# Attention products of a pair of heads in three runs on the matrix engine instead of four

## The chip, the cores and the metric

The kernel runs on one core of one Trainium2 chip. The metric is the device time of one execution in microseconds. Three executions of the kernel before took 984.92, 981.54 and 982.50 us; the median is 982.5 us.

## What is computed

The output is two results side by side. Result A is an attention with a compressive memory: 2048 positions of 576 features, 32 heads of 18 features, in four segments of 512 positions. Result B is the real part of a two-dimensional Fourier transform, written as products with cosine and sine matrices. Cut to what matters:

```python
for s in range(N):                      # N = 4 segments of L = 512 positions
    logits = qs @ ks.T * scale + mask   # per head, causal
    a_dot = softmax(logits) @ vs
    o = g * (pq @ M) / (pq @ z + 1e-6) + (1 - g) * a_dot
    M, z = M + pk.T @ vs, z + pk.sum()  # pq = phi(qs), pk = phi(ks)
A = concat(o) @ wo
a, b = x @ dft_hid_re.T, x @ dft_hid_im.T
B = dft_seq_re @ a - dft_seq_im @ b     # 2048 x 2048 times 2048 x 576, twice
```

## The kernel before, in words

The program has three stages. The first projects queries, keys and values and keeps the memory sums; the last is the output projection `output_stage`. The stage between them, from about 218 us to 918 us of the trace, holds the change. There the program writes two streams of work into one another by hand.

The **dense stream** is result B, in the generator `dense`. Its matmuls are `d<-wide,chi`, `d<-wide,clo` and the like (L584, and L629 to L634 in `hidden`): stationary blocks of 128x128 and 288 moving columns, both of 4-byte numbers. A high part `chi` is cut by ScalarE and a low part `clo` by GpSimd, and the output tiles `d` have three banks of PSUM.

The **attention stream** is the generator `attention`, one turn for each of the 64 pairs of heads and four more turns to empty the pipeline. Its matmuls have 2-byte operands. Of pair p it handles several ages at once: the even head's score products for the row maxima are made at age 0, the odd head's scores at age 2 (`F_LAG`), the even head's transposed scores at age 3 (`T_LAG`) and the value sums `pv` of both heads at age 4 (`V_LAG`).

- `s_fill(n, kind)`: the even head's score products of one `kind` by `scores` (L969), and the row minima on VectorE by `smallest` (L975), into `negm`. There are three kinds, which together cover the causal triangle: kind 0 is one product of 512 columns, kind 1 is two products of 128 and 384 columns, kind 2 is one product of 256 columns.
- `f_fill(n, kind)`: the same for the odd head, into `nb`; its scores stay in PSUM until `f_exp` reads them on ScalarE. Kind 0 goes to a bank of the tag `t`, the others to a bank of `s`.
- `t_fill(n, kind)`: the even head's transposed scores in a bank of `t` (L1046, L1051, L1055, L1056), and their exponentials on ScalarE. `t_lo` makes the low halves `plo`; of kind 1 it reads the bank itself (L1078, VectorE).
- `pv(n)`: 20 products of 55 and 37 columns for one head (L1095, L1096). The weights are `phi` and `plo` for the even head and the transposed `ptt` for the odd one.

The tags `s` and `t` have two banks each, taken in turn by `bank`. Each new tile must wait until the readers of the bank's last tile are done.

A turn has eight slots. Each slot emits its attention work and then yields a weight from `SLOTS`; the loop that calls it then emits dense matmuls until the dense share of the work has caught up. So the attention products come in **runs**, with dense matmuls between them. In the kernel before a turn has four: slot 2 (`s_fill` 0 and 1, `t_fill` 0 and 1), slot 4 (value sums of the even head, then `s_fill` 2), slot 5 (`f_fill` 1, `t_fill` 2, `f_fill` 0) and slot 7 (value sums of the odd head, then `f_fill` 2). Where the dense stream is ahead, nothing is emitted after slot 4, and the runs of slots 4 and 5 stand together.

Of the kernel before, what the change touches and what calls it, by code (L numbers as in the profile page):

```python
# [12 lines left out]
F32 = mybir.dt.float32  # L13
# [9 lines left out]
S, D, H, DH, NSEG, L = 2048, 576, 32, 18, 4, 512  # L23
P = 128
# [16 lines left out]
def infini_attention_and_fnet(ctx: ExitStack, tc: tile.TileContext, xT, wqk, w8, wv, wo, beta, xtT, cT, hT, out):  # L41
# [46 lines left out]
    def later(n, fn, *a):  # L88
        due.setdefault(clock[0] + n, []).append((fn, a))
# [113 lines left out]
    for i in range(2):  # L203
        kn.append(tuple(sk.tile([P, D], F32R, name=f"kn{n}{i}") for n in "hl"))
        t = sk.tile([P, 2, H, 19], F32R, name=f"vn{i}")
# [3 lines left out]
    for i in range(3):  # L209
        t = sb.tile([P, H, 55], BF16, name=f"vs{i}")  # L210
# [253 lines left out]
    def stacks(p_, i):  # L464
        qs_bufs.append(p_.tile([P, 4, L], BF16, name=f"qs{i}"))
        ks_bufs.append(p_.tile([P, 4, L], BF16, name=f"ks{i}"))
        pool.memset(ks_bufs[i].bitcast(F32)[96:], BF16_ONES)

    CAUSAL, NEGM, MB, OG = [], [], [], []
# [18 lines left out]
    def stack_load(G):  # L488
        if G < NG:
            s, g8 = divmod(G, 8)  # L490
            rows = slice(g8 * 72, g8 * 72 + 72)
            for n, (buf, src) in enumerate(((ks_bufs, kd), (qs_bufs, qd))):
                later(1 + n, dma, buf[G % 4][:NPAIR], src[s][rows].rearrange("(h d) c t -> (d c) h t", d=DH))
# [71 lines left out]
    def bank(name, shape, dtype, tag):  # L565
        turns[tag] ^= 1
        return ps.tile(shape, dtype, name=name, tag=f"{tag}{turns[tag]}", bufs=1)
# [392 lines left out]
    ROWS = (((3, 0),), ((0, 384), (2, 0)), ((1, 0),))  # L960
    FIRST_COL = {3: 0, 2: 512, 0: 896, 1: 1024}

    def scores(n, kind, tag="s"):
        G, h = divmod(n, 4)
        q, k = qs_bufs[G % 4][:NPAIR, h], ks_bufs[G % 4][:NPAIR, h]
        o = bank("s", [P, L], F32, tag)
        for i, c in ROWS[kind]:
            w = (i + 1) * P
            pe.matmul(o[:, c:c + w], q[:, i * P:w], k[:, :w], start=True, stop=True)  # L969
        return o  # L970

    def smallest(o, kind, scale, into):
        for i, c in ROWS[kind]:
            w = (i + 1) * P
            dve.tensor_tensor_reduce(o[:, c:c + w], o[:, c:c + w], CAUSAL[0][:, L - w:], scale=scale, scalar=-LOWEST,  # L975
                                     op0=OP.add, op1=OP.min, accum_out=into[:, i:i + 1])

    def s_fill(n, kind):
        G, h = divmod(n, 4)
        smallest(scores(n, kind), kind, -1.0, NEGM[G % 2][:, 2 * h:2 * h + 4])  # L980

    F_ = {}

    def f_fill(n, kind):
        o = scores(n, kind, "s" if kind else "t")
        if kind == 1:
            F_[n] = [sa.tile([P, 4], F32, name="nb", bufs=2), sa.tile([P, 1280], F32, name="pf", bufs=3), {}]
        smallest(o, kind, -SCALE, F_[n][0])
        F_[n][2][kind] = o
# [28 lines left out]
    def maxima(G):  # L1018
        m, b = NEGM[G % 2].rearrange("p (h n) -> p h n", h=2), MB[G % 2][:, :24].rearrange("p (h c n) -> p c h n", h=2, c=3)
        r = sa.tile([P, 2, 4], F32, name="negx", bufs=2)  # L1020
        pool.tensor_copy(b[:, 0], m)
        pool.tensor_tensor(r, m, b[:, 0], OP.subtract)
        pool.tensor_copy(b[:, 1], r)
        pool.tensor_tensor(b[:, 2], r, b[:, 1], OP.subtract)

    def maxima_transpose(G, o):
        t = o[:, 384:512]
        pe.matmul(t, MB[G % 2], ident16, start=True, stop=True)
        yield
        w = sa.tile([24, P], BF16, name="mt", bufs=2)  # L1030
        act.activation(w, t[:24], AF.Copy)
        for h in range(2):
            later(1, dma, qs_bufs[G % 4][NPAIR:NPAIR + 3, 2 * h].rearrange("c (n t) -> c n t", n=4), w[12 * h:12 * h + 12])
# [64 lines left out]
    def pv_out(n2):  # L1098
        G, hh = divmod(n2, 2)
        s, g8 = divmod(G, 8)  # L1100
        o = PV.pop(n2)
        og = OG[G % 2]
        h0 = 4 * g8 + 2 * hh
        w = o[:, 440:].rearrange("p (h i c) -> p h i c", h=2, c=1)
        b = o[:, :144].rearrange("p (h i d) -> p h i d", h=2, i=4)
        o = o[:, :440].rearrange("p (h i c) -> p h i c", h=2, i=4)
        a = sa.tile([P, 8, DH], F32, name="pa", bufs=2)
        dve.reciprocal(w, o[:, :, :, 54:])
        dve.tensor_tensor(w, w, g1[:, h0:h0 + 2, None, None].to_broadcast([P, 2, 4, 1]), OP.mult)
        dve.tensor_reduce(a, o[:, :, :, :54].rearrange("p h i (c d) -> p (h i) d c", c=3), axis=AX, op=OP.add)  # L1110
        to = og[:, :, 36 * hh:36 * hh + 36].rearrange("p i (h d) -> p h i d", d=DH)
        a = a.rearrange("p (h i) d -> p h i d", h=2)
        if s == 0:
            dve.tensor_tensor(to, a, w.to_broadcast([P, 2, 4, DH]), OP.mult)
        else:
            dve.tensor_tensor(b, a, w.to_broadcast([P, 2, 4, DH]), OP.mult)
            dve.tensor_tensor(to, to, b, OP.add)
        if hh == 1:
            later(6, turn_out, G)
# [33 lines left out]
    F_LAG, T_LAG, V_LAG = 2, 3, 4  # L1153
    NP = 2 * NG
    SLOTS = (1060.0, 890.0, 1060.0, 660.0, 890.0, 1060.0, 650.0, 1210.0)

    def attention():
        for p in range(NP + V_LAG):
            def even(lag, fn, *a):
                if 0 <= p - lag < NP:  # L1160
                    fn(2 * (p - lag), *a)

            def odd(lag, fn, *a):
                if 0 <= p - lag < NP:
                    fn(2 * (p - lag) + 1, *a)

            if p < 2:
                OG.append(sa.tile([P, 4, 72], F32, name=f"og{p}"))
            if p == 0:
                stack_load(1)  # L1170
                later(20, value_load, 0)
            if p % 2 == 0:
                later(39, value_load, p // 2 + 1)
                later(30, memory_load, p // 2)
            even(T_LAG + 1, t_lo, 0)
            odd(F_LAG + 1, f_split_hi)
            yield SLOTS[0]
            G = p // 2 - 1 if p % 2 == 0 and 0 < p <= NP else None
            even(0, s_fill, 0)
            even(T_LAG, t_fill, 0)  # L1180
            even(T_LAG, t_fill, 1, G)
            even(0, s_fill, 1)
            if G is not None and p < T_LAG:
                list(maxima_transpose(G, bank("trm", [P, L], F32, "t")))
            odd(F_LAG + 1, f_split_lo, pool, 512, 1280)
            yield SLOTS[1]
            even(T_LAG, t_lo, 1)
            odd(F_LAG + 1, f_split_lo, dve, 0, 512)
            yield SLOTS[2]
            even(V_LAG, pv)  # L1190
            if p < 2:
                stacks(sq, p + 2)
            even(0, s_fill, 2)
            even(T_LAG, t_mask)
            yield SLOTS[3]
            odd(F_LAG, f_fill, 1)
            even(T_LAG, t_fill, 2)
            odd(F_LAG, f_fill, 0)
            if p % 2 and p < NP:
                maxima(p // 2)  # L1200
            yield SLOTS[4]
            odd(F_LAG + 1, f_turn)
            if p % 2:
                if p == 1:
                    later(6, stack_load, 2)
                else:
                    stack_load((p + 3) // 2)
                if 2 < p < 18:
                    later(2, copy_parts, 2, 7 + p // 2)
            elif 4 <= p < 36:  # L1210
                later(2, copy_parts, 3, (p - 4) // 2)
            even(T_LAG, t_hi)
            yield SLOTS[5]
            odd(V_LAG, pv)
            odd(F_LAG, f_fill, 2)
            odd(F_LAG, f_exp, 1)
            even(T_LAG, t_lo, 2)
            yield SLOTS[6]
            odd(F_LAG, f_exp, 0, 2)
            if V_LAG <= p < NP + V_LAG - 1:  # L1220
                pv_out(p - V_LAG)
            yield SLOTS[7]
# [8 lines left out]
    for n, w in enumerate(attention()):  # L1231
        tick()
        ta += w
        for fn, a in PLAN.pop(n, ()):
            fn(*a)
        while td / total_d < ta / total_a:
            t = next(d, BREAK)
            if t is BREAK:
                break
            td += t  # L1240
# [56 lines left out]
```

## Time and profile before

| | |
|---|---|
| median of three executions | 982.5 us |
| the profiled execution | 981.44 us |
| its span in the trace | 979.7 us |
| busy: TensorE matmuls, weight loads | 974.2 us, 916.4 us |
| busy: VectorE, ScalarE, GpSimd | 742.1 us, 702.2 us, 661.4 us |
| granted TensorE clock | 0.999 of full |

The span is what the trace covers, 1.7 us less than the execution's own time. TensorE's matmuls are listed with a start and a duration; they are pipelined and their ends are modelled, so neighbours overlap in the list and the busy time says little. What counts is the time from one start to another with a known number of matmuls between them.

### The profile page before, as it was taken

To read this page: it belongs to the slowest core of one execution; us is meant where nothing else is said; L and a number is where in the kernel's file an instruction comes from. 1 tells how busy PE (TensorE), PEld (TensorE's weight loads), DVE (VectorE), ACT (ScalarE), POOL (GpSimd) and SP (SyncE) were. 2 spreads that over 40 slices of the span, in tenths; PEclk is the share of its full clock that TensorE was granted. 3 is DMA by queue.
4 is the path that set the end of the run, shared out by engine and by line. 5 is a ranking of instruction groups with operands and counts; after the bars stand their busy time and mean duration, and the time that the engine had idled before them with its cause. 6 is when DMAs were issued, how large, how long until landed. Compare 5 with 4: busy or idle time off the path is not lost.

```text
span 979.7 us, 25347 instructions
## 1 busy us (share of the span) xinstructions
PE 974.2 (99%) x9246; PEld 916.4 (94%) x9246; DVE 742.1 (76%) x2113; ACT 702.2 (72%) x1623; POOL 661.4 (68%) x746
## 2 busy tenths in 40 slices
PE   9999999999999999999999999999999999999998
PEld 8989989899999999999999999999999999999998
DVE  6657668585677767777888777787888798887884
ACT  6757576564877777878878787877777777778442
POOL 2658577686766766677676776667667986677561
PEclk9999999999999999999999999999999999999999
DMA  7537556775777999889999999889999999988662
GB/s 243 197 117 244 200 169 247 236 249 175 203 185 204 217 240 239 220 213 244 222 251 244 236 207 203 184 197 226 233 240 257 249 243 233 226 206 186 174 206 107
DMA packets 304349, 209.95 MB, mean 214 GB/s; under 512 B 204992, under 2 KB 259136, under 8 KB 304192
## 3 DMA queue, kind: packets, MB, share of 16 engines
q1 hardware_dynamic: 304000, 208.20, 82.6%
q8 instruction: 72, 1.18, 0.5%
q14 instruction: 53, 0.43, 0.1%
q10 hardware_dynamic: 224, 0.14, 0.0%
HBM read 122.37 MB, written 58.98 MB: 185 GB/s over the span
## 4 chain that ended last, share of the span: by engine, by line
PE 99%; ACT 0%; DVE 0%; issue 0%
PE d L584 42%; PE s L969 7%; PE v L84 6%; PE qk L84 6%; PE qk L251 6%; PE pv L1095 4%; PE d L629 4%; PE d L630 3%; PE d L631 3%; PE pv L1096 2%; PE t L869 2%; PE d L869 2%; PE s L869 2%; PE t L1046 1%; PE m L364 1%; PE look L397 1%
## 5 line engine op out<-in xcount | busy, mean ns | idle before, releaser
L975 DVE CUSTOM_DVE_ANT_0 s<-s,causal 128x128 f32<-128x128 f32 (+3 forms) x512 | 249.8, 504 | 103.6 <-PE s L969 97.0
L457 POOL TENSOR_TENSOR clo<-craw,chi 128x512 fp32r<-128x512 f32 x159 | 217.0, 1365 | 107.3 <-ACT chi L452 91.9
L584 PE MATMUL d<-wide,chi 128*128 128x288 f32 x1408 | 260.1, 302 | 0.0
L584 PEld LDWEIGHTS d<-wide,chi 128*128 128x128 f32 x1408 | 210.5, 188 | 0.7
L584 PE MATMUL d<-wide,clo 128*128 128x288 f32 x704 | 171.2, 310 | 0.0
L1011 POOL TENSOR_TENSOR hl<-pf,hl 128x768 f16<-128x768 f32 x64 | 107.7, 1683 | 66.7 <-ACT hl L1007 54.2
L969 PE MATMUL s<-ks,qs 108*128 108x128 bf16 (+3 forms) x512 | 131.6, 301 | 0.0
L1059 ACT ACTIVATE phi<-t 128x384 f16<-128x384 f32 x128 | 61.9, 483 | 90.9 <-PE t L1056 90.7
L998 ACT ACTIVATE pf<-s,nb 128x128 f32<-128x128 f32 (+3 forms) x256 | 121.0, 524 | 4.2
L584 PE MATMUL d<-ab,chi 128*128 128x288 f32 x640 | 122.3, 300 | 0.0
L584 PEld LDWEIGHTS d<-wide,clo 128*128 128x128 f32 x704 | 117.7, 188 | 0.9
L452 ACT ACTIVATE chi<-craw 128x512 fp32r<-128x512 f32 x160 | 100.0, 625 | 2.8 <-DMA craw<-cT 1.2
L584 PEld LDWEIGHTS d<-ab,chi 128*128 128x128 f32 x640 | 97.6, 188 | 0.3
L1007 ACT ACTIVATE hl<-pf 128x768 f16<-128x768 f32 (+1 forms) x128 | 87.3, 732 | 1.0
L584 PE MATMUL d<-ab,clo 128*128 128x288 f32 x320 | 82.4, 306 | 0.0
L629 PE MATMUL d<-wide,chi 128*128 128x288 f32 x256 | 79.7, 311 | 0.0
L630 PE MATMUL d<-wide,chi 128*128 128x288 f32 x256 | 75.6, 295 | 0.0
L631 PE MATMUL d<-wide,clo 128*128 128x288 f32 x256 | 75.5, 295 | 0.0
L1063 ACT ACTIVATE pf<-t 128x512 f32<-128x512 f32 (+1 forms) x128 | 68.9, 538 | 1.6 <-PE t L1046 1.4
L1078 POOL TENSOR_TENSOR plo<-pf,phi 128x384 f16<-128x384 f32 x64 | 60.9, 952 | 11.2 <-ACT pf L1063 9.0
L289 POOL TENSOR_TENSOR p<-r,p 128x512 bf16<-128x512 f32 x36 | 43.4, 1209 | 22.2 <-ACT p L288 20.9
L969 PEld LDWEIGHTS <-qs 108*128 108x128 bf16 x512 | 44.3, 97 | 13.8 <-issue 0.2
(286 smaller groups left out, 2584.9 us busy)
## 6 DMA issues: line engine op xcount, KB each, us to landing
craw<-cT SPq DMA_DIRECT2D x128, 256.0 KB
ks<-kd SPq DMA_DIRECT2D x32, 432.0 KB
qs<-qd SPq DMA_DIRECT2D x32, 432.0 KB
craw<-xtT SPq DMA_DIRECT2D x32, 320.0 KB
vd<-vs SPq DMA_DIRECT2D x16, 440.0 KB
vst<-vd SPq DMA_DIRECT2D x32, 220.0 KB
qd<-p SPq DMA_DIRECT2D x16, 384.0 KB
kd<-p SPq DMA_DIRECT2D x16, 384.0 KB
```

The source lines that it names most:

```text
L84: pe.matmul(o, a, b, start=n == 0, stop=n == len(terms) - 1)
L452: act.activation(hi, raw[:, :4], AF.Copy)
L457: engine.tensor_tensor(lo, raw[:, :4], hi.bitcast(F32), OP.subtract)
L584: pe.matmul(o[h], a, b[:, h * 288:h * 288 + 288], start=start, stop=stop)
L629: pe.matmul(o, xh[:, k], wl[k][:, cs], start=k == 0, stop=False)
L630: pe.matmul(o, xh[:, k], wh[k][:, cs], start=False, stop=False)
L631: pe.matmul(o, xl[:, k], wh[k][:, cs], start=False, stop=False)
L969: pe.matmul(o[:, c:c + w], q[:, i * P:w], k[:, :w], start=True, stop=True)
L975: dve.tensor_tensor_reduce(o[:, c:c + w], o[:, c:c + w], CAUSAL[0][:, L - w:], scale=scale, scalar=-LOWEST, op0=OP.add, op1=OP.min, accum_ ...
L998: act.activation(f[:, FIRST_COL[i]:FIRST_COL[i] + w], o[kind][:, c:c + w], AF.Exp, bias=nb[:, i:i + 1], scale=-1.0)
L1007: act.activation(hl[:, 0, a:b], f[:, a:b], AF.Copy)
L1011: engine.tensor_tensor(hl[:, 1, a:b], f[:, a:b], hl[:, 0, a:b], OP.subtract)
```

## The change

Three moves within a turn. The value sums of the even head go from slot 4 to the end of slot 5. The even head's 256 columns (`s_fill` 2) and the odd head's (`f_fill` 2, before in slot 7) go into slot 5 as well, directly after `f_fill` 1, and share one `s` bank: the even head's in its first half, the odd head's in its second. VectorE's minima of the two follow in slot 5. `maxima` goes from slot 5 to slot 6. `SLOTS` is not changed.

```diff
+    SHARED = []
+
     def scores(n, kind, tag="s"):
         G, h = divmod(n, 4)
         q, k = qs_bufs[G % 4][:NPAIR, h], ks_bufs[G % 4][:NPAIR, h]
-        o = bank("s", [P, L], F32, tag)
+        if kind == 2 and SHARED:
+            o = SHARED.pop()
+        else:
+            o = bank("s", [P, L], F32, tag)
+            if kind == 2:
+                SHARED.append(o[:, 256:])
...
             even(T_LAG, t_lo, 1)
             odd(F_LAG + 1, f_split_lo, dve, 0, 512)
             yield SLOTS[2]
-            even(V_LAG, pv)
             if p < 2:
                 stacks(sq, p + 2)
-            even(0, s_fill, 2)
             even(T_LAG, t_mask)
             yield SLOTS[3]
+            SHARED.clear()
+            both = {}
             odd(F_LAG, f_fill, 1)
+            even(0, lambda n: both.update(s=scores(n, 2)))
+            odd(F_LAG, lambda n: both.update(f=scores(n, 2)))
+            even(0, lambda n: s_fill(n, 2, both["s"]))
             even(T_LAG, t_fill, 2)
             odd(F_LAG, f_fill, 0)
+            odd(F_LAG, lambda n: f_fill(n, 2, both["f"]))
+            even(V_LAG, pv)
+            yield SLOTS[4]
             if p % 2 and p < NP:
                 maxima(p // 2)
-            yield SLOTS[4]
             odd(F_LAG + 1, f_turn)
...
             yield SLOTS[5]
             odd(V_LAG, pv)
-            odd(F_LAG, f_fill, 2)
             odd(F_LAG, f_exp, 1)
```

`s_fill` and `f_fill` take the filled bank as an argument where it is given.

**TensorE, end of the run of slot 4, before** (turn 18; `s_6280` is the even head's 256 columns, `d_5996` the dense stream):

```order
L1095 LDWEIGHTS phi_6025
L1095 MATMUL pv_6259<-vst_5982,phi_6025 128x55
L1096 LDWEIGHTS plo_6026
L1096 MATMUL pv_6259<-vst_5982,plo_6026 128x37
L969 LDWEIGHTS qs1_2774
L969 MATMUL s_6280<-ks1_2775,qs1_2774 128x256
L584 MATMUL d_5996<-ab_3830,chi_6121 128x288
```

The even head's value sums end, the 256 columns follow, and the dense stream comes back. The run of slot 7 ends in the same way with the odd head's 256 columns. In the changed kernel, the end of the even head's value sums in the same turn:

```order
L1103 LDWEIGHTS phi_6010
L1103 MATMUL pv_6272<-vst_5967,phi_6010 128x55
L1104 LDWEIGHTS plo_6011
L1104 MATMUL pv_6272<-vst_5967,plo_6011 128x37
L584 MATMUL d_6301<-wide_2869,chi_6180 128x288
L584 MATMUL d_6301<-wide_2868,chi_6180 128x288
```

Here the dense stream follows a value sum of 37 columns. The run of slot 7 now ends so too, with `ptt` as the weights.

**TensorE, the run of slot 5, before** (the odd head's scores are `s_6292` and `s_6304`, the even head's transposed scores `t_6299`):

```order
L584 MATMUL d_5996<-ab_3939,clo_6122 128x288
L969 LDWEIGHTS qs0_2430
L969 MATMUL s_6292<-ks0_2431,qs0_2430 128x128
L969 LDWEIGHTS qs0_2430
L969 MATMUL s_6292<-ks0_2431,qs0_2430 128x384
L1055 LDWEIGHTS ks3_3055
L1055 MATMUL t_6299<-qs3_3054,ks3_3055 128x128
L1056 LDWEIGHTS ks3_3055
L1056 MATMUL t_6299<-qs3_3054,ks3_3055 128x256
L969 LDWEIGHTS qs0_2430
L969 MATMUL s_6304<-ks0_2431,qs0_2430 128x512
L584 MATMUL d_6315<-wide_2869,chi_6196 128x288
```

And in the changed kernel, from the product of 384 columns on (`s_6259` is the shared bank):

```order
L976 MATMUL s_6252<-ks0_2431,qs0_2430 128x384
L976 LDWEIGHTS qs1_2774
L976 MATMUL s_6259<-ks1_2775,qs1_2774 128x256
L976 LDWEIGHTS qs0_2430
L976 MATMUL s_6259<-ks0_2431,qs0_2430 128x256
L1063 LDWEIGHTS ks3_3055
L1063 MATMUL t_6263<-qs3_3054,ks3_3055 128x128
L1064 LDWEIGHTS ks3_3055
L1064 MATMUL t_6263<-qs3_3054,ks3_3055 128x256
L976 LDWEIGHTS qs0_2430
L976 MATMUL s_6268<-ks0_2431,qs0_2430 128x512
L1103 LDWEIGHTS phi_6010
```

Both products of 256 columns now stand inside the run, and the product of 512 columns is followed by the value sums. Over the whole program the order has these runs. Before: 116 of value sums ending in 256 columns, 57 of slot 5 alone, 6 of slots 4 and 5 together, 5 of value sums alone. After: 60 of slot 5 with both products of 256 columns and the value sums, 2 with one of them, and 65 of value sums alone.

**VectorE, the same turn, before** (each row of minima is followed by a row that reads the result out):

```order
L1078 TENSOR_TENSOR plo_6215<-t_6223,phi_6214 128x384
L1011 TENSOR_TENSOR hl_6193<-pf_6103,hl_6193 128x512
L975 ISA s_6280,negm1_2424<-s_6280,causal_2421 128x256
L975 ISA negm1_2424 128x1
L975 ISA s_6292,nb_6295<-s_6292,causal_2421 128x128
L975 ISA nb_6295 128x1
L975 ISA s_6292,nb_6295<-s_6292,causal_2421 128x384
L975 ISA nb_6295 128x1
L975 ISA s_6304,nb_6295<-s_6304,causal_2421 128x512
L975 ISA nb_6295 128x1
L1130 STREAM_TRANSPOSE ogt_6307<-og0_2866 128x128 x2
L975 ISA s_6351,nb_6295<-s_6351,causal_2421 128x256
```

And in the changed kernel:

```order
L1086 TENSOR_TENSOR plo_6199<-t_6207,phi_6198 128x384
L1019 TENSOR_TENSOR hl_6177<-pf_6064,hl_6177 128x512
L982 ISA s_6252,nb_6255<-s_6252,causal_2421 128x128
L982 ISA nb_6255 128x1
L982 ISA s_6252,nb_6255<-s_6252,causal_2421 128x384
L982 ISA nb_6255 128x1
L982 ISA s_6259,negm1_2424<-s_6259,causal_2421 128x256
L982 ISA negm1_2424 128x1
L982 ISA s_6268,nb_6255<-s_6268,causal_2421 128x512
L982 ISA nb_6255 128x1
L982 ISA s_6259,nb_6255<-s_6259,causal_2421 128x256
L982 ISA nb_6255 128x1
```

The even head's minimum of 256 columns moves behind the odd head's first two, and the odd head's moves up ahead of the transposes, from slot 7 into slot 5.

More of the change, by code (lines that the diff above doesn't have):

```diff
@@ L976, in smallest, with s_fill, f_fill @@
                                      op0=OP.add, op1=OP.min, accum_out=into[:, i:i + 1])
-    def s_fill(n, kind):
+    def s_fill(n, kind, o=None):
         G, h = divmod(n, 4)
-        smallest(scores(n, kind), kind, -1.0, NEGM[G % 2][:, 2 * h:2 * h + 4])
+        smallest(scores(n, kind) if o is None else o, kind, -1.0, NEGM[G % 2][:, 2 * h:2 * h + 4])
     F_ = {}
-    def f_fill(n, kind):
-        o = scores(n, kind, "s" if kind else "t")
+    def f_fill(n, kind, o=None):
+        if o is None:
+            o = scores(n, kind, "s" if kind else "t")
         if kind == 1:
```

## The prediction

> **What bounds the kernel now.** I read the page's first and fourth parts, and then the table of TensorE's waits.
>
> ```profile
> span 979.7 us, 25347 instructions
> PE 974.2 (99%) x9246; PEld 916.4 (94%) x9246; DVE 742.1 (76%) x2113; ACT 702.2 (72%) x1623; POOL 661.4 (68%) x746
> PE 99%; ACT 0%; DVE 0%; issue 0%
> PE warm L240 <- DVE ones L68: 1.1, 1, 1.1
> ```
>
> The chain that ended last is TensorE for 99% of the span, and the last row is the whole table of its waits: 1.1 us at the start. Nothing else that the profile shows held it up. So the time is the sum of what TensorE does, whatever the other engines do in their free quarter. A change can gain only by making TensorE's sequence shorter, and loses by making it longer or by adding a wait. No matmul is added or removed here; only neighbours change. The question is therefore what a neighbour costs, and since modelled ends overlap, I read it from starts in the timeline.
>
> Here are a run of slot 4 (value sums and 256 columns) and the next run of slot 5, columns start and modelled length:
>
> ```profile
> 500.22 0.20 PE L1095 MATMUL pv<-vst,phi 128*128 128x55 bf16 x1
> ...
> 500.72 0.18 PE L1096 MATMUL pv<-vst,plo 128*128 128x37 bf16 x1
> 500.75 0.27 PE L969 MATMUL s<-ks,qs 108*128 108x256 bf16 x1
> 500.77 0.78 PE L584 MATMUL d<-wide,chi 128*128 128x288 f32 x4
> 501.39 0.39 PE L969 MATMUL s<-ks,qs 108*128 108x128 bf16 x2
> 501.62 0.22 PE L1055 MATMUL t<-qs,ks 111*128 111x128 bf16 x1
> 501.68 0.27 PE L1056 MATMUL t<-qs,ks 111*128 111x256 bf16 x1
> 501.79 0.38 PE L969 MATMUL s<-ks,qs 108*128 108x512 bf16 x1
> 501.82 0.62 PE L584 MATMUL d<-wide,clo 128*128 128x288 f32 x2
> 502.27 0.70 PE L584 MATMUL d<-wide,chi 128*128 128x288 f32 x4
> 502.81 0.43 PE L584 MATMUL d<-wide,clo 128*128 128x288 f32 x2
> 503.07 0.69 PE L584 MATMUL d<-wide,chi 128*128 128x288 f32 x4
> ```
>
> Dense pace: from 502.27 to 503.07 there are 6 matmuls in 0.80 us, 0.133 each. The run of slot 4 takes from 500.22 to 501.39, 1.17 us, with 4 dense matmuls in it; 1.17 - 0.533 = **0.637 us** is the run's own. The run of slot 5 and two dense matmuls take from 501.39 to 502.27: 0.88 - 0.267 = **0.613 us**. A run of value sums alone stands near the end of the stage, where no score products are left:
>
> ```profile
> 895.92 0.20 PE L1095 MATMUL pv<-vst,phi 128*128 128x55 bf16 x1
> ...
> 896.41 0.18 PE L1096 MATMUL pv<-vst,plo 128*128 128x37 bf16 x1
> 896.44 0.78 PE L584 MATMUL d<-wide,chi 128*128 128x288 f32 x4
> 897.06 0.43 PE L584 MATMUL d<-wide,clo 128*128 128x288 f32 x2
> 897.33 0.39 PE L969 MATMUL s<-ks,qs 108*128 108x128 bf16 x2
> ```
>
> It takes 1.41 us with 6 dense matmuls, so **0.61 us** of its own. This is the row that decides the case: at the end of the value sums, 256 more columns cost only 0.637 - 0.61 = 0.027 us. The return from a 37-column product to the dense stream has dead time in it, and the 256 columns fill that dead time.
>
> **The change part by part.**
>
> *(a) The 256-column products go inside a run.* There they follow and are followed by products with 2-byte operands. In the rows above a 256-column product inside a run (501.68) is followed after 0.11 us (501.79). So each one that loses its place at the end of the value sums costs 0.11 instead of 0.027, or 0.083 more. The order has 116 of these: 116 x 0.083 = **+9.6 us**. Nothing hides it, since TensorE is the path. The pair 256 after 256 into one bank isn't in the trace before. From below I bound it by half of the 512 columns at the end of a run (from 501.79 to 502.27 are 0.48 us; less two dense matmuls that is 0.213, and half of it 0.107), and from above by 0.11 plus the 0.017 of (b). I take 0.11, the row of the same size. That makes (a) 9.3 to 11.6 us.
>
> *(b) The 512-column product is no longer last.* At the end of the run it costs the 0.213 us just worked out. Inside a run:
>
> ```profile
> 507.42 0.39 PE L969 MATMUL s<-ks,qs 108*128 108x512 bf16 x1
> 507.65 0.39 PE L1046 MATMUL t<-qs,ks 111*128 111x128 bf16 x4
> ```
>
> it is followed after 0.23 us, 0.017 more. The value sums behind it aren't in the trace as its neighbour; the nearest bounds are 0.213 and 0.23, and I take the latter, which is also between two products inside a run. 62 x 0.017 = **+1.1 us**. The Trainium skill, "TensorE: Matmul & The Clock Gate", section "Back-to-back issue gap", states some 131 ns for 512 columns in a stream of pairs of weight load and matmul; by it this term would be about 62 x -0.08 = -5 us (an estimate) and the sum half as large. The 0.23 us row, which has a weight load behind it, disagrees, and I go by the row.
>
> *(c) One return to the dense stream less per turn.* Six times the kernel before has slots 4 and 5 in one run, one of them here:
>
> ```profile
> 480.35 0.20 PE L1095 MATMUL pv<-vst,phi 128*128 128x55 bf16 x1
> ...
> 480.88 0.49 PE L969 MATMUL s<-ks,qs 108*128 108x256 bf16 x3
> ...
> 481.40 0.62 PE L584 MATMUL d<-wide,chi 128*128 128x288 f32 x2
> 481.86 0.30 PE L584 MATMUL d<-wide,clo 128*128 128x288 f32 x1
> ```
>
> From 480.35 to 481.86 are 1.51 us with two dense matmuls: 1.51 - 0.267 = 1.243 us for both, against 0.637 + 0.613 = 1.250 in two runs. So a return saved is worth about 0.007 us when the run saved ended in 256 columns; part of it was their dead time, which (a) counts. I put 60 x -0.003 = **-0.2 us**, between nothing and this row. The 65 value-sum runs of slot 7 and the 62 of slot 5 now end bare, at the 0.61 us above, which (a) has counted by the 0.027.
>
> *(d) New waits of TensorE.* Slot 5 begins sooner behind slot 2, because the 0.637 us run of slot 4 between them is gone. It still needs VectorE to have finished slot 2's work: the shared bank needs the even head's minima of kind 1, and the odd head's 512 columns need `plo<-t`, which reads that bank. Mostly this was done long before:
>
> ```profile
> 418.21 0.56 DVE L1078 TENSOR_TENSOR plo<-t,phi 128x384 f16<-128x384 f32 x1
> 419.94 0.39 PE L969 MATMUL s<-ks,qs 108*128 108x128 bf16 x2
> 420.33 0.38 PE L969 MATMUL s<-ks,qs 108*128 108x512 bf16 x1
> ```
>
> The 512 columns at 420.33 would come 0.637 sooner and two products of 0.11 later, at 419.91; `plo` is done at 418.77, 1.14 us ahead. But VectorE is late where its copy `plo<-pf` is drawn out:
>
> ```profile
> 753.07 1.78 DVE L1078 TENSOR_TENSOR plo<-pf,phi 128x512 f16<-128x512 f32 x1
> 756.28 0.14 DVE L975 DVE_READ_ACCUMULATOR2_ANT negm<- 128x1 f32 x1
> 756.48 0.39 PE L969 MATMUL s<-ks,qs 108*128 108x128 bf16 x2
> 823.82 2.14 DVE L1078 TENSOR_TENSOR plo<-pf,phi 128x512 f16<-128x512 f32 x1
> 874.35 1.70 DVE L1078 TENSOR_TENSOR plo<-pf,phi 128x512 f16<-128x512 f32 x1
> ```
>
> Here the minima are read out until 756.42. Slot 5 would begin at 756.48 - 0.64 = 755.84, and its shared bank would be asked for after the products of 128 and 384 columns (0.23 us by 501.39 to 501.62) at 756.07: TensorE waits 0.35 us. Behind the waiting matmul stand the rest of the run and the whole dense stream. I count the three turns quoted, and take the other two to be like this one: 3 x 0.35 = **+1.1 us**, between 0 (VectorE may be ahead by then) and some 4 us, which is a dozen such turns.
>
> *(e) What costs nothing.* VectorE's minima only change places; TensorE doesn't wait for them within the turn. The odd head's last minimum moves ahead of its exponentials by two slots, so ScalarE can only have it sooner. `maxima` is four short GpSimd operations, due in the second slot of the next turn, three slots and more later. If that cover is gone, the 24-column transpose waits and with it TensorE, as in (d). The value sums come later than their operands by a slot more than before. The only DMA near a moved step is `f_turn`, which keeps its place in slot 6, so nothing is moved past SP's queue.
>
> The sum is 9.6 + 1.1 - 0.2 + 1.1 = **+11.6 us**. The profiled execution took 981.44 us (span 979.7 and 1.7 around it), so the changed kernel would take 993.0 in such an execution. The median of the three runs is 1.06 above it, so I predict **994.0 us**.
>
> **The rivals.**
>
> *Waits of VectorE in every fourth turn.* Slot 5 now hands VectorE five minima in a row, and slots 2 to 5 lie closer together. If the lag of 0.35 us comes back in 16 turns of 64, (d) is 5.6 instead of 1.1 and the time 998.5. For it: VectorE is busy for 76% of the span, and for its late copies. Against: the 1.14 us of room in the ordinary turn.
>
> *The 256 columns cost the same everywhere.* A return to the dense stream may have no dead time, and a product then costs its columns in either place. Then (a) is 0 and the time 982.5 + 1.1 - 0.2 + 1.1 = 984.5 us, no change that can be seen. For it: in the dense stream itself the weight loads are hidden, 0.133 us a matmul. Against it stands the bare run: 0.61 us beside 0.637. The Trainium skill, same page, section "Step-by-step: what each phase is for", says that the next tile's weights are loaded while the matmul before still runs, which would give this rival's result; the bare run disagrees where the matmul before is as short as 37 columns.
>
> *Faster: a fixed price for each return.* The first dense pair after a run is listed with 0.62 us (501.82) where an ordinary pair has 0.43 (502.81). If these 0.19 us were a price of the change of operand type, paid once a return whatever ends the run, then 60 returns less would give -11.4 us. Moving the 256 columns would be free, since they fill nothing, and with (d) the time would be 982.5 - 11.4 + 1.1 = 972.2 us. From some 0.16 us a return on (9.6 / 60) it would outweigh even (a). Against it: the six runs that already stand together save 0.007 us, not 0.19. The 0.19 is just the 512 columns still streaming, 0.213 by (b).
>
> That the change doesn't do what it says is excluded by the order of the instructions, which has 60 of the long runs.
>
> **How the numbers follow.** My forecast, 994.0, gets 0.82; the waits in every fourth turn 0.10; no change 0.04; the fixed price 0.04. Beside the predicted value stands what the bounds allow: low 9.3 + 1.1 - 0.2 + 0 = 10.2, and a run lies up to 1.0 below the median, 982.5 + 10.2 - 1.0 = 991.7; the starts are rounded to 0.01 us, which on 116 products is over 1 us more, so 990.0. High: 11.6 + 1.1 + 4 = 16.7, or 999.2, and I go to 1000.0, which takes in the first rival. The two on the other side, 8 in 100 together, are left out. Taking 0.3% (2.9 us) as about what a measurement of this kernel can tell from no change, the chances are 0.04 faster, 0.04 the same, 0.92 slower.
>
> **What would show it.** In the trace after, a run of slot 5 ought to take 0.613 + 2 x 0.11 + 0.017 + 0.61, about 1.46 us, and the run of slot 7 0.61. Between the two products of 256 columns should lie 0.11 us. TensorE's waits should hold a few rows of VectorE with about 1 us in total. The prediction is wrong if a run that ends bare takes as little as 0.52 us (20 products at the 0.026 between 500.22 and 500.72), if the second 256 columns come nearly free, or if TensorE shows waits of over 4 us.

## The result and the profile after

The changed kernel takes 992.22 us (median of five, 991.64 to 992.64), the kernel before 982.93 us in the five runs beside it. The ratio is 1.0088, with a 95% interval of 1.0074 to 1.0103: slower by 9.3 us. The prediction was 994.0 us, between 990.0 and 1000.0. The profiled execution took 991.64 us, 10.2 more than the one before.

The page's head, its chain and the whole table of TensorE's waits, after:

```profile
span 989.9 us, 25262 instructions
PE 984.2 (99%) x9246; PEld 923.1 (93%) x9246; DVE 761.6 (77%) x2113; ACT 702.1 (71%) x1623; POOL 666.6 (67%) x746
PE 99%; DVE 0%; ACT 0%; issue 0%
```

```profile
PE warm L240 <- DVE ones L68: 1.1, 1, 1.1
PE s L976 <- DVE negm L982: 0.2, 1, 0.2
```

TensorE has the same 9246 matmuls, is still the chain, and shows one new wait of 0.2 us. So its sequence itself has become longer, by about 10 us. The timeline of TensorE has the place, a run of slot 5 and the next of slot 7:

```profile
504.41 0.61 PE L976 MATMUL s<-ks,qs 108*128 108x128 bf16 x4
504.86 0.22 PE L1063 MATMUL t<-qs,ks 111*128 111x128 bf16 x1
504.92 0.27 PE L1064 MATMUL t<-qs,ks 111*128 111x256 bf16 x1
505.03 0.38 PE L976 MATMUL s<-ks,qs 108*128 108x512 bf16 x1
505.25 0.19 PE L1103 MATMUL pv<-vst,phi 128*128 128x55 bf16 x1
...
505.76 0.51 PE L584 MATMUL d<-wide,clo 128*128 128x288 f32 x2
506.11 0.70 PE L584 MATMUL d<-wide,chi 128*128 128x288 f32 x4
...
507.71 0.20 PE L1103 MATMUL pv<-vst,ptt 128*128 128x55 bf16 x1
...
508.25 0.78 PE L584 MATMUL d<-wide,chi 128*128 128x288 f32 x4
508.87 0.43 PE L584 MATMUL d<-wide,clo 128*128 128x288 f32 x2
```

Four score products (128, 384 and twice 256 columns) take 0.45 us up to 504.86. The first two took 0.23 before, so each 256-column product costs 0.11 here. The 512 columns are followed by the value sums after 0.22 us. From 504.41 to 506.11 are 1.70 us; less two dense matmuls at 0.133 the run takes 1.43 us. The run of slot 7 takes 1.16 - 0.533 = 0.63 us, nearly the 0.637 it took before *with* 256 columns at its end. That is the loss: the product moved away, and the run that it left became hardly shorter.

### The profile page after: what moved, and what is told of

The parts are those of the page before. It is cut to its first block, busy times and chain, and to the rows that moved or that the text cites. A ratio compares the mean times of both kernels' runs of the same rounds, so it can differ in the third digit from the quotient of the medians.

```text
span 989.9 us, 25262 instructions
## 1 busy us (share of the span) xinstructions
PE 984.2 (99%) x9246; PEld 923.1 (93%) x9246; DVE 761.6 (77%) x2113; ACT 702.1 (71%) x1623; POOL 666.6 (67%) x746
## 4 chain that ended last, share of the span: by engine, by line
PE 99%; DVE 0%; ACT 0%; issue 0%
PE d L584 42%; PE s L976 7%; PE v L84 6%; PE qk L84 6%; PE qk L251 6%; PE pv L1103 4%; PE d L629 4%; PE d L630 3%; PE d L631 3%; PE pv L1104 2%; PE t L869 2%; PE d L869 2%; PE s L869 1%; PE m L364 1%; PE t L1054 1%; PE look L397 1%
## 5 line engine op out<-in xcount | busy, mean ns | idle before, releaser
L457 POOL TENSOR_TENSOR clo<-craw,chi 128x512 fp32r<-128x512 f32 x159 | 219.3, 1379 | 107.3 <-ACT chi L452 83.2
L982 DVE CUSTOM_DVE_ANT_0 s<-s,causal 128x128 f32<-128x128 f32 (+3 forms) x512 | 243.9, 511 | 49.5 <-PE s L976 44.3
L584 PE MATMUL d<-wide,chi 128*128 128x288 f32 x1408 | 256.6, 299 | 0.0
L584 PE MATMUL d<-wide,clo 128*128 128x288 f32 x704 | 167.6, 305 | 0.0
L1019 POOL TENSOR_TENSOR hl<-pf,hl 128x768 f16<-128x768 f32 x64 | 116.3, 1817 | 48.1 <-ACT hl L1015 38.3
L976 PE MATMUL s<-ks,qs 108*128 108x128 bf16 (+3 forms) x512 | 112.8, 302 | 0.2 <-DVE negm L982 0.2
L629 PE MATMUL d<-wide,chi 128*128 128x288 f32 x256 | 78.0, 305 | 0.0
L630 PE MATMUL d<-wide,chi 128*128 128x288 f32 x256 | 75.6, 295 | 0.0
L631 PE MATMUL d<-wide,clo 128*128 128x288 f32 x256 | 75.6, 295 | 0.0
L1086 DVE TENSOR_TENSOR plo<-pf,phi 128x512 f16<-128x512 f32 x64 | 73.4, 1147 | 0.0
L976 PEld LDWEIGHTS <-qs 108*128 108x128 bf16 x512 | 41.9, 98 | 18.4 <-issue 0.7
```

Of the source, the lines that this page charges most:

```text
L457: engine.tensor_tensor(lo, raw[:, :4], hi.bitcast(F32), OP.subtract)
L584: pe.matmul(o[h], a, b[:, h * 288:h * 288 + 288], start=start, stop=stop)
L629: pe.matmul(o, xh[:, k], wl[k][:, cs], start=k == 0, stop=False)
L630: pe.matmul(o, xh[:, k], wh[k][:, cs], start=False, stop=False)
L631: pe.matmul(o, xl[:, k], wh[k][:, cs], start=False, stop=False)
L1019: engine.tensor_tensor(hl[:, 1, a:b], f[:, a:b], hl[:, 0, a:b], OP.subtract)
```

## The experiments

The theory behind the prediction: when the dense stream comes back, TensorE stands still for about 0.11 us from the start of the last short product, and 256 columns at that place fill the time. Its rivals were that the long run itself costs, that each return has a fixed price, and that the stop belongs to the change of operand type. All six kernels compute the whole result.

### e1_swap_only: the 256 columns ahead of the value sums, nothing merged

```diff
-            even(V_LAG, pv)
...
             even(0, s_fill, 2)
+            even(V_LAG, pv)
...
-            odd(V_LAG, pv)
             odd(F_LAG, f_fill, 2)
+            odd(V_LAG, pv)
```

> The kernel before with four runs a turn, but the 256-column products stand ahead of the value sums instead of behind them, so the runs of slots 4 and 7 end bare. Theory (on the return to the dense stream TensorE stands still for about 0.11 us from the start of the last short product, and 256 columns placed there fill that time): 116 x 0.083 = +9.6 us, 992.5 us, ratio 1.010, with nothing merged. Rival (the long run costs the time, not the place of the 256 columns): no long run is made, so 983 us, ratio 1.000.

Measured: 993.46 us, ratio 1.0109 (1.0096 to 1.0122), 10.5 us more than before. A run of slot 4 in its timeline:

```profile
504.86 0.28 PE L969 MATMUL s<-ks,qs 108*128 108x256 bf16 x1
504.98 0.19 PE L1095 MATMUL pv<-vst,phi 128*128 128x55 bf16 x1
...
505.49 0.77 PE L584 MATMUL d<-wide,chi 128*128 128x288 f32 x4
506.11 0.39 PE L969 MATMUL s<-ks,qs 108*128 108x128 bf16 x2
```

From 504.86 to 506.11 are 1.25 us with 4 dense matmuls, so the run takes 0.72 us, where the same products in the other order took 0.637. The 0.08 us on 116 runs are 9.3 to 9.6 us. Read in the same way for all 116 runs of the two traces, the means are 0.720 and 0.631 us, which makes 10.3 us, near the 10.5 measured; the 256 columns at the head of a run take 0.12 us here (504.86 to 504.98), not 0.11. Swapping neighbours, with no run merged, costs as much as the whole change. The rival that the long run is to blame falls.

### e2_three_covered: three runs, each with 256 columns behind its value sums

The odd head's 256 columns stay at the end of slot 7. The even head's bank is taken at the start of slot 5, its product comes last. As in the change, `maxima` goes to slot 6 (not shown):

```diff
-            even(V_LAG, pv)
...
-            even(0, s_fill, 2)
...
             yield SLOTS[3]
+            early = []
+            even(0, lambda n: early.append(bank("s", [P, L], F32, "s")))
             odd(F_LAG, f_fill, 1)
             even(T_LAG, t_fill, 2)
             odd(F_LAG, f_fill, 0)
+            even(V_LAG, pv)
+            even(0, lambda n: s_fill(n, 2, early[0]))
```

> Three runs a turn as in the change, but each run that ends in value sums has a 256-column product behind them: the even head's at the end of slot 5, the odd head's at the end of slot 7. Theory: every return is covered again, so about 983 us (982.3 to 983.5), ratio 1.000; the return saved is worth 60 x 0.007 = 0.4 us at most. Rival (the long run itself costs): 990 us or more, ratio 1.008. Second rival (a fixed price of 0.19 us for each return): 60 x 0.19 = 11.4 us less, 971.5 us, ratio 0.988.

Measured: 983.42 us, ratio 1.0014 (1.0005 to 1.0024). One return less per turn, as in the change, and 8.8 us of the loss are gone. So the long run does not cost what its rival said (990 us or more). The fixed price of a return is excluded, since 971.5 us would be far off. A long run in its timeline:

```profile
500.65 0.39 PE L969 MATMUL s<-ks,qs 108*128 108x128 bf16 x2
...
501.79 0.27 PE L969 MATMUL s<-ks,qs 108*128 108x256 bf16 x1
501.81 0.51 PE L584 MATMUL d<-wide,clo 128*128 128x288 f32 x2
502.16 0.70 PE L584 MATMUL d<-wide,chi 128*128 128x288 f32 x4
```

It takes 1.51 - 0.267 = 1.243 us, against 0.637 + 0.613 = 1.250 in two runs before: the saving foretold, some 0.4 us over the program. Against it stand 0.9 us of new waits for VectorE, which TensorE's table has in this execution:

```profile
PE s L969 <- DVE negm L975: 0.6, 2, 0.4
PE s L969 <- DVE plo L1078: 0.3, 1, 0.3
```

That these waits make the difference to the kernel before was not shown: the medians differ by 0.5 us, and the interval of the ratio puts the difference between 0.5 and 2.4 us.

### e3_512_last: the changed kernel with the 512 columns behind the value sums

```diff
-            odd(F_LAG, f_fill, 0)
-            odd(F_LAG, lambda n: f_fill(n, 2, both["f"]))
             even(V_LAG, pv)
+            odd(F_LAG, f_fill, 0)
+            odd(F_LAG, lambda n: f_fill(n, 2, both["f"]))
```

> The changed kernel with the value sums of slot 5 ahead of the odd head's 512 columns, so that the 512 columns end the long run; slot 7 still ends bare. Theory: 62 returns are covered again, each worth 0.11 - 0.026 + 0.006 = 0.09 us, so 5.5 us less than the changed kernel, about 986.8 us, ratio 1.004. Rival (the long run itself costs): as the changed kernel, 992 us, ratio 1.009.

Measured: 986.31 us, ratio 1.0035 (1.0023 to 1.0047), 5.9 us less than the changed kernel. The long run has the same products as there, with both 256-column products inside it; only the order at its end has changed. From its timeline:

```profile
503.11 0.61 PE L976 MATMUL s<-ks,qs 108*128 108x128 bf16 x4
...
504.25 0.38 PE L976 MATMUL s<-ks,qs 108*128 108x512 bf16 x1
504.27 0.62 PE L584 MATMUL d<-wide,clo 128*128 128x288 f32 x2
504.73 0.70 PE L584 MATMUL d<-wide,chi 128*128 128x288 f32 x4
```

1.62 - 0.267 = 1.353 us instead of 1.433: 0.08 us less on each of 62 runs, 5.0 us of the 5.9.

### e4_two_of_128: the 256 columns as two products of 128

In `scores` of the kernel before:

```diff
-            pe.matmul(o[:, c:c + w], q[:, i * P:w], k[:, :w], start=True, stop=True)
+            for a in ((0, P) if i == 1 else (0,)):
+                e = a + P if i == 1 else w
+                pe.matmul(o[:, c + a:c + e], q[:, i * P:w], k[:, a:e], start=True, stop=True)
```

> The kernel before with each 256-column product written as two products of 128 columns, in the same place, with the same result. Theory (the stop lasts 0.11 us from the start of the last short product, as long as a weight load of the dense stream): the first 128 columns cost 0.055 us and the second fills only half of the stop, so 116 x 0.055 = +6.4 us, about 989.3 us, ratio 1.0065. Rival (the stop belongs to the value sums, and any product behind them of 256 columns in all fills it): +0.3 to +0.6 us for 128 more instructions, ratio 1.000 to 1.001.

Measured: 989.58 us, ratio 1.0071 (1.0058 to 1.0083), 6.7 us more. From its timeline, the end of a run of slot 4:

```profile
503.41 0.18 PE L1098 MATMUL pv<-vst,plo 128*128 128x37 bf16 x1
503.43 0.27 PE L971 MATMUL s<-ks,qs 108*128 108x128 bf16 x2
503.51 0.77 PE L584 MATMUL d<-wide,chi 128*128 128x288 f32 x4
504.13 0.39 PE L971 MATMUL s<-ks,qs 108*128 108x128 bf16 x2
```

From 503.43 to 504.13 are 0.70 us, less 4 dense matmuls 0.17: the first 128 columns at about 0.055, then 0.11 from the start of the second to the dense stream. One product of 256 columns there took 0.64 - 0.533 = 0.11 (500.75 to 501.39 before). Behind a value sum of 37 columns it is nearly the same: in the prediction's rows of a bare run, 896.41 to 897.06 are 0.65 us, or 0.12 without the 4 dense matmuls (0.533). So the stop runs from the start of the *last* product, whichever of these it is. The rival falls.

### e5_short_dense: short products within the dense stream

In `hidden`, for the second transform only, each product of 288 columns of L629 to L631 becomes two of 144:

```diff
-                pe.matmul(o, xh[:, k], wl[k][:, cs], start=k == 0, stop=False)
-                pe.matmul(o, xh[:, k], wh[k][:, cs], start=False, stop=False)
-                pe.matmul(o, xl[:, k], wh[k][:, cs], start=False, stop=False)
+                for n, (a, b) in enumerate(((xh, wl), (xh, wh), (xl, wh))):
+                    for c in (0, 144) if ri else (0,):
+                        e = c + 144 if ri else 288
+                        pe.matmul(o[:, c:e], a[:, k], b[k][:, h * 288 + c:h * 288 + e], start=k + n + c == 0, stop=False,
+                                  skip_group_check=ri == 1)
```

> The kernel before, with 384 of the dense matmuls (the 4-byte products of the second hidden transform, 288 columns each) written as two of 144 columns, with the same result. No type of operand changes next to them. Theory (a matmul with 4-byte weights can't start sooner than about 0.11 us after the one before it, however short that one is): 384 x (2 x 0.11 - 0.133) = +33 us, about 1016 us, ratio 1.034. Rival (the stop of 0.11 us belongs to the change from 2-byte to 4-byte operands, and short 4-byte products go at the speed of their columns): 144 columns then take about 0.073 us (by the pace of 0.133 for 288 and 0.227 for 512 columns), so 384 x 0.013 = +5 us, 988 us, ratio 1.005.

Measured: 1017.11 us, ratio 1.0356 (1.0341 to 1.0372), 35 us more, where the two sides had 33 and 5. From its timeline:

```profile
601.55 0.61 PE L632 MATMUL d<-wide,chi 128*128 128x144 f32 x4
602.00 0.39 PE L632 MATMUL d<-wide,clo 128*128 128x144 f32 x2
602.22 0.61 PE L632 MATMUL d<-wide,chi 128*128 128x144 f32 x4
```

Six products from 601.55 to 602.22 take 0.67 us, 0.112 each, with no 2-byte product near them. The kernel before has the same pace in the timeline of its first stage, where the memory lookup multiplies 152 columns of 4-byte numbers, five of them from 99.62 to 100.18 in 0.56 us:

```profile
99.62 0.39 PE L397 MATMUL look<-md,pq_hi 128*128 128x152 f32 x2
99.84 0.27 PE L397 MATMUL look<-md,pq_lo 128*128 128x152 f32 x1
99.95 0.39 PE L397 MATMUL look<-md,pq_hi 128*128 128x152 f32 x2
100.18 0.28 PE L397 MATMUL look<-md,pq_lo 128*128 128x152 f32 x1
```

So a stop of this size needs no change of type. At every place read so far, a matmul with 128 columns of 4-byte weights starts its work at least 0.11 us after the matmul before it began. The natural reading is its weight load, which the trace lists as an instruction of its own, 188 ns of listed length against 97 for 2-byte weights. The kernel before has a place that speaks for it: the memory sums of its first stage, where one block of weights has 64 columns and not 128 (`128*64`):

```profile
42.90 0.24 PE L364 MATMUL m<-vn,knh 128*64 128x152 f32 x1
42.98 0.38 PE L364 MATMUL m<-vn,knl 128*128 128x152 f32 x2
```

The next product starts 0.08 us later (in most of the twelve such places 0.07), where a product of the same 152 columns took 0.112 us with 128 columns of weights. With half the weights to load, the floor of 0.11 is gone. No run changed the weights alone at a return to the dense stream.

The Trainium skill, "TensorE: Matmul & The Clock Gate", section "LDWEIGHTS (loading the stationary operand)", has about columns / 1.2 ns, or 107 ns for 128 columns (an estimate by its formula); the 112 ns agree with it for 4-byte weights. The value sums, each with its own load of 128 columns of 2-byte weights, follow one another after 26 ns, so those load much faster.

### e6_three_512_last: another order with every return covered

```diff
             yield SLOTS[3]
+            even(0, s_fill, 2)
             odd(F_LAG, f_fill, 1)
             even(T_LAG, t_fill, 2)
-            odd(F_LAG, f_fill, 0)
+            even(V_LAG, pv)
+            odd(F_LAG, f_fill, 0)
```

The value sums and `s_fill` 2 leave slot 4, and `maxima` goes to slot 6, as in the change.

> Three runs a turn, all covered: slot 5 has the even head's 256 columns, the odd head's 128 and 384, the transposed scores, the value sums and last the odd head's 512 columns; slot 7 ends in the odd head's 256 columns. Theory: the run of slot 5 takes 0.613 + 0.524 + 0.11 = 1.247 us against 0.637 + 0.613 = 1.250 before, so no gain and no loss, 982.5 to 983.2 us, ratio 1.000. Rival (a long run costs something of its own, as the 0.5 us of the three covered runs might say): 983.5 us or more, ratio over 1.001.

Measured: 983.57 us, ratio 1.0011 (1.0002 to 1.0020). Covered in another way, it comes out where e2 does, 8.7 us below the changed kernel, and about 1 us slower than before, not faster. By the numbers this is the rival's outcome (983.5 us or more) and not the theory's (up to 983.2). But a long run in its timeline is no longer than foretold:

```profile
500.61 0.50 PE L969 MATMUL s<-ks,qs 108*128 108x256 bf16 x3
...
501.66 0.61 PE L584 MATMUL d<-wide,clo 128*128 128x288 f32 x2
502.11 0.69 PE L584 MATMUL d<-wide,chi 128*128 128x288 f32 x4
```

It takes 1.50 - 0.267 = 1.233 us, where the theory had 1.247 and the two runs before 1.250. What is new is in the table of TensorE's waits:

```profile
PE t L1046 <- DMA qs<-mt: 1.1, 2, 0.8
PE s L969 <- DVE negm L975: 0.3, 1, 0.3
```

The rows of maxima (`mt`) reach TensorE late twice in this execution, and a third new wait of 0.3 us stands in the first stage. Together they are 1.7 us of the 1.9 by which this profiled execution (983.33 us) is longer than the one before. That the other executions have the same waits was not shown. Moving `maxima` is not needed for a late `mt`: e5, which leaves it in place, has one such wait of 0.7 us.

No version beats the kernel before, and the theory gives no more than the 0.4 us of e2: there, all but five returns behind value sums are covered already.

## Why the prediction was right

**The bound** held: TensorE is 99% of the chain before and after, and in e1, e3 and e4. In e2, e5 and e6 it is 95, 98 and 92%, as the chain there runs back through other engines and DMA; TensorE is busy for 99% of the span in these too.

**(a), the 256 columns inside a run, +9.6 us,** was right in mechanism and size. The 256 after 256 into one bank, not seen before, cost the 0.11 us taken for it (0.22 for the two). e1 shows the term alone, with 10.5 us, and e2 and e6 take it away. The prediction spoke of dead time on a return without saying what it is; e4 shows that it is counted from the last product's start, and e5 that the same 0.11 us stand between 4-byte products alone.

**(b), the 512 columns inside a run, +1.1 us,** was too large. Before the value sums they take 0.22 us and not 0.23, so 62 x 0.007 = 0.4 us. The row taken was the one with a 128-column product behind it; the lower bound was nearer.

**(c), one return less, -0.2 us,** had the right size, as far as starts rounded to 0.01 us can tell: e2's long run takes 1.243 us against 1.250.

**(d), new waits, +1.1 us,** was too large. One such place came, 0.2 us in the table, in another turn than the three quoted. It has the cause foretold, VectorE's drawn-out `plo<-pf` ahead of the minima; VectorE's timeline after:

```profile
811.39 2.18 DVE L1086 TENSOR_TENSOR plo<-pf,phi 128x512 f16<-128x512 f32 x1
814.89 0.57 DVE L982 CUSTOM_DVE_ANT_0 s<-s,causal 128x384 f32<-128x384 f32 x1
815.37 0.14 DVE L982 DVE_READ_ACCUMULATOR2_ANT negm<- 128x1 f32 x1
```

and TensorE's at the same place:

```profile
814.93 0.39 PE L976 MATMUL s<-ks,qs 108*128 108x128 bf16 x2
815.56 0.38 PE L976 MATMUL s<-ks,qs 108*128 108x256 bf16 x2 [0.24 <-DVE negm L982]
```

The minima are read out until 815.51, and the shared bank's first product starts at 815.56: 0.63 us behind 814.93 instead of 0.23, so the stop is 0.40 us, of which the table counts 0.24 as waiting. At the three places quoted, TensorE did not wait; why VectorE was in time there was not looked into. The ground of the first rival did come: `plo<-pf` on VectorE took 1.15 us in the mean of its 64 executions after the change, and 0.78 before. In e3, which keeps the change's order of minima, it took 1.05, in e2 and e6 0.82 and 0.79. Only one became a wait, so the room that a turn has, 1.14 us in the one read for the prediction, was mostly enough.

With the measured sizes the sum is 9.6 + 0.4 - 0.2 + 0.4 = 10.2 us, which is the difference of the two profiled executions. That it agrees to 0.1 us is luck, as a start misread by 0.01 us is over 1 us on 116 products. In the medians the difference is 9.3 us, because the profiled execution before lay 1.5 us below its median and the one after 0.6. The forecast was 1.8 us too high: 1.4 of it come from (b) and (d), each 0.7 too large, and the rest from the 1.06 us that it put between such an execution and the median.

## What to carry to other kernels

When short 2-byte products are woven into a stream of 4-byte matmuls, let each group end in a product of at least some 0.11 us (256 columns here), and put the very short ones ahead of it; grouping more of them together is worth next to nothing by itself. Before a product is moved, ask what it was hiding where it stood: its price there was 0.027 us, and inside a group 0.11. Starts in the timeline show this. TensorE's busy time grew by the same 10 us (974.2 to 984.2) without saying where, and the listed length of the dense `d<-wide,chi` even fell, from 302 to 299 ns.

## What the runs showed of the hardware

Matmuls with 4-byte operands of 144 columns went at 0.112 us each, and those of 288 columns at 0.133; halving a product's columns made the pair 0.09 us dearer. With 64 columns of weights in place of 128, 152 columns went in 0.07 to 0.08 us and not in 0.112. Products with 2-byte weights have no such floor at this length: 128 columns in 0.055 us and value sums of 37 and 55 columns in 0.026. VectorE's 128x512 subtraction that makes `plo`, 0.78 us in the mean of the kernel before and 1.15 in the changed one, took up to 2.18 us in single cases; no run here looked for the cause.
